# Fused attention and feed-forward kernel: one PSUM bank serves the attention scores first and layer one later

## The chip, the cores and the metric

The kernel runs on one core of one Trainium2 chip. The metric is the device time of one execution in microseconds (us); below the time, the traced span from the first to the last instruction is used, which is a little shorter. A difference is stated between medians of several executions.

The core has a matrix engine (TensorE, PE in the profile; loading its stationary operand is PEld), a vector engine (DVE), a scalar engine (ACT), a general engine (POOL) and a queue that issues the transfers (SP). Matrix products land in PSUM, which this kernel divides into eight banks of 128 partitions by 512 four-byte values.

## The reference, cut to what matters

```python
# 8 batches, 8 heads, 576 positions, head size 64
scores = q @ k.T / 8
cum    = cumsum(maximum(s, 0))
scores = where(causal, -1e9, scores + minimum(cum_k - cum_q, 0))
attn   = softmax(scores)
x      = (attn @ v) laid out as 4608 tokens x 512
h      = x @ w_in                      # 512 x 2048, "layer one"
g      = where(h > 0, h, exp(minimum(h, 0)) - 1)
out    = g @ w_out                     # 2048 x 512, "layer two"
```

## The kernel before

The program is written by a planner. Each piece of work is an `op` with a list of engines that could do it and what it costs there by a table, what it reads and writes, and a priority (smaller is more urgent). `Plan.issue` keeps a clock for each engine, repeatedly takes the operation that can start first (priority breaks ties) and appends its instructions. So the order on every engine is fixed when the program is built, each engine then runs its list in that order, and a small change in a rule reorders everything behind it. `plan.now` is the planned clock of TensorE. Times in the planner's table order the work; they aren't measurements.

**Attention** runs over batches and, within a batch, over pairs of heads `j` = 0 to 3. The first three batches begin with a *low* part of 320 positions in plain four-byte arithmetic (tiles `kl`, `ql`, `early`). A low unit makes five score tiles `sc` (one of 128 columns, two of 192, two of 320). A DVE instruction (L1144) adds the mask, takes the minimum `mn` and so frees the score bank; ACT exponentiates; the rows are normalised; then TensorE transposes them (`trl`), a copy brings them to `tl`, and the product with the values goes to `avl`. The remaining work, five whole batches and the late positions of the first three, splits operands in two parts (`sc<-kh,qs` and `sc<-k,q`), transposes by transfer (`T`), and has one small tile for each pair of heads and batch that covers the first 64 positions (names with `None`). The outputs become the tokens `x_first` (the first 512 tokens) and `x`.

**The network** takes 256 tokens at a time, 18 chunks. For each chunk it makes eight tiles `h` of layer one (two blocks of 128 features by 256 tokens, one PSUM bank), passes each through ACT and DVE to `g` and `gg`, and accumulates layer two in `o`. The first two chunks are native four-byte (L1447 and L1477, weights `wv`), the other sixteen use sums of three half-precision products (L1506 and L1566, weights `wp`). A chunk whose tokens come from two batches is first brought to one scale (L1411). The weights arrive as eight-byte words in `w_raw` and are decoded by ACT (L707) and DVE (L710 and L712), 1024 columns an instruction.

**Filler.** While the planned TensorE clock is under 60 us (`FILL_T`), a planned TensorE gap of more than 0.35 us (`GAP`) is filled with transposes of the identity into `scratch` (L1623), up to 300 of them. They compute nothing that is used.

**PSUM banks.** Eight are shared out by tags: `a` two (scores and transposes), `av` one, `h` three, `o` two. A tile may also name other tags with a rule; with `always=True` the planner may use them at any time the rule allows. Before, the score tiles name `h` and `o` under the rule `plan.now < OPEN_T`, and `OPEN_T` is 0.

Of the kernel before, what the change touches and what calls it, by code (L numbers as in the profile page):

```python
# [9 lines left out]
F32 = mybir.dt.float32  # L10
# [7 lines left out]
P = 128  # L18
# [6 lines left out]
SMALLEST = 2.0**-12  # L25
TOP, DOWN = 13, 22

N_ST, N_A, N_AV, N_H, N_O, N_IO, N_G, N_GG, N_X, N_T, N_K, N_V = 2, 2, 1, 3, 2, 2, 1, 3, 2, 2, 2, 2
TC = 256
NATIVE = 2  # L30
TX = 512
# [3 lines left out]

V_AHEAD = 30

FIRST_T, OPEN_T = 180e3, 0.0

DYN_T = 300e3  # L40

# [253 lines left out]
def pe4(n):  # L295

    return 4 * pe(n)
# [7 lines left out]
def act_c(n):  # L305

    return 165 + n / 1.2
# [36 lines left out]
def kernel(  # L344
# [39 lines left out]
    ps = ctx.enter_context(tc.tile_pool(name="ps", bufs=1, space=bass.MemoryType.PSUM))  # L384

    plan = Plan(tc)
# [183 lines left out]
    for n in range(NF // 2):  # L570
        tag = f"wa_{n}" if n < 4 else f"wp_{n // 2 - 1}"
# [8 lines left out]
    def weight(f, kind):  # L580
        t, at = w_values[f // 2]
        return (t, (f, kind)), lambda: t.v[:, at + f % 2, kind]
# [189 lines left out]
    for b, blocks in pieces:  # L772
        late = blocks[0] > 0
        start[b, late] = at
        n = P * len(blocks) + HB * (not late)
# [5 lines left out]
    def domains(ch):  # L781
# [5 lines left out]
                   others=[(f"wa_{m}", 1, lambda n: n > 0) for m in range(2)], always=True)  # L787
# [147 lines left out]
    def weighing_low(u):  # L935
        prio, n = u.prio + 1, CUT * P
        wide = P + 2 * n + sum(2 * (HB + P * i) for i in range(CUT))
        turned = plan.buf(sb, [P, wide], F32, f"tl_{u.tag}", tag="T", bufs=N_T)
        av = plan.buf(ps, [P, 512], F32, f"avl_{u.tag}", tag="av", bufs=N_AV)
        ends = [P]  # L940

        def pair():
            tr = plan.buf(ps, [P, 512], F32, f"trl_{u.tag}", tag="a", bufs=N_A)
            op(prio, [("PE", 111.0, lambda: pe_.transpose(tr.v[:, :P], u.first.v, ident))], [u.first], [tr],
               late=[low_scale[u.b]] if u.b in low_scale else ())
            psum_copy(prio, P, lambda: turned.v[:, :P], lambda: tr.v[:, :P], [tr], [(turned, "pair")])

            def products():
                for h in range(2):
                    pe_.matmul(av.v[h * HB : (h + 1) * HB, :HB], u.vs_of()[:, 0], turned.v[:, h * HB : (h + 1) * HB],  # L950
                               start=True, stop=True)

            op(prio, [("PE", 2 * pe4(HB), products)], [(turned, "pair"), u.vs], [av])

        def keys(kb):

            tr = plan.buf(ps, [P, 512], F32, f"trl_{u.tag}_{kb}", tag="a", bufs=N_A)
            i0, half = max(kb - 1, 0), kb > 0
            m, c = CUT - i0, P * (CUT - i0) - HB * half

            def turns():
                for h in range(2):
                    for i in range(i0, CUT):
                        o = (h * m + i - i0) * P
                        pe_.transpose(tr.v[:, o : o + P], u.pp[h, i].v[:, kb * P : (kb + 1) * P], ident)

            op(prio, [("PE", 222.0 * m, turns)], [u.pp[h, i] for h in range(2) for i in range(i0, CUT)], [tr],
               late=[low_scale[u.b]] if u.b in low_scale else ())
            at, = ends
            ends[0] = at + 2 * c  # L970

            def dst():
                return turned.v[:, at : at + 2 * c].rearrange("p (h q) -> p h q", h=2)

            psum_copy(prio, 2 * c, dst,
                      lambda: tr.v[:, : 2 * m * P].rearrange("p (h q) -> p h q", h=2)[:, :, m * P - c :],
                      [tr], [(turned, kb)])

            def products():
                for h in range(2):  # L980
                    pe_.matmul(av.v[h * HB : (h + 1) * HB, LOW - c : LOW], u.vs_of()[:, 1 + 2 * kb + h], dst()[:, h],
                               start=kb == 0, stop=kb == CUT)

            op(prio, [("PE", pe4(c), products)], [(turned, kb), u.vs], [av])
            if kb < CUT:
                return
            col = S_LOW + 2 * u.b
            produce(prio, u.j, start[u.b, False], LOW, lambda: av.v[:, :LOW],
                    [av] + ([(scales, col)] if u.b in low_scale else []),
                    lambda: scales.v[:, col : col + 1])  # L990

        return [pair] + [lambda kb=kb: keys(kb) for kb in range(CUT + 1)]
# [126 lines left out]

    plan.signal = (id(ps), "o")  # L1120

    def score_bank(name):

        def opening(n):
            return plan.now < OPEN_T

        return plan.buf(ps, [P, 512], F32, name, tag="a", bufs=N_A,
                        others=[("h", N_H, opening), ("o", N_O, opening)], always=True)

    def softmax_block(prio, tag, native, pt, w, mask, mv, reads, operands, inv, view=lambda v: v):  # L1130

# [297 lines left out]
    def network():  # L1429
# [10 lines left out]
        def hidden_native(ch, fp):  # L1440

            side = -1000
            hp = plan.buf(ps, [P, 2, TC], F32, f"h_{ch}_{fp}", tag="h", bufs=N_H)
            lo, up = ch * TC, ch * TC + TC
            for m in range(2):
                for c in range(NCB):
                    op(main(ch), [("PE", pe4(TC), lambda m=m, c=c: pe_.matmul(  # L1447
                        hp.v[:, m], weight(2 * fp + m, 0)[1]()[:, c * P : (c + 1) * P], x_first.v[:, c, lo:up],
                        start=c == 0, stop=c == NCB - 1))],
                       [(x_first, (j, a)) for a, e, j in x_spans if j == c and a < up and e > lo] + [weight(2 * fp + m, 0)[0]], [hp])  # L1450
            gt = plan.buf(sb, [P, 2 * TC], F32, f"g_{ch}_{fp}", tag="g", bufs=N_G)
            op(side, [("ACT", act_c(2 * TC), lambda: act.activation(gt.v, flat(hp.v), AF.Exp))], [hp], [gt])
            sign = [False]

            def negative():
                act.activation(gt.v, gt.v, AF.Relu, bias=1.0, scale=-1.0)
                sign[0] = True

            op(side, [
                ("DVE-SB", dve_1(2 * TC), lambda: dve.tensor_scalar(gt.v, gt.v, 1.0, -1.0, ALU.min, ALU.add)),  # L1460
                ("ACT", act_s(2 * TC), negative),
            ], [], [gt])
            gg = plan.buf(sb, [P, 2, TC], F32, f"gg_{ch}_{fp}", tag="gg", bufs=N_GG)
            op(side, [("DVE", dve_p(2 * TC), lambda: dve.scalar_tensor_tensor(
                flat(gg.v), flat(hp.v), 0.0, gt.v, ALU.max, ALU.subtract if sign[0] else ALU.add))],
               [gt, hp], [gg])
            return gg
# [19 lines left out]
        def hidden(n):  # L1487

            ch, fp = steps[n]
# [6 lines left out]
                group_constants(ch, cs[ch])  # L1496
            x, o = xs[ch * TC // TX], ch * TC % TX
            parts = [p for p in x_parts[ch * TC // TX] if p[0] < ch * TC + TC and p[1] > ch * TC]
            hp = plan.buf(ps, [P, 2, TC], F32, f"h_{ch}_{fp}", tag="h", bufs=N_H)
            for m in range(2):  # L1500
                f = 2 * fp + m
                for c in range(NCB):
# [202 lines left out]
```

## Time and profile before

| what | value |
|---|---|
| median of 3 runs | 1055.4 us (1053.96 to 1056.38) |
| the profiled execution: time, span | 1054.67 us, 1052.9 us |
| TensorE busy | 1031.1 us (98%) |
| DVE, ACT, POOL busy | 831.8, 623.3, 426.4 us |
| mean granted TensorE clock | 0.997 |

"Busy" for TensorE comes from modelled ends of matmuls that overlap in the pipeline, so the mean time of one is longer than the step from one to the next; where a price of one matmul is wanted, starts of successive rows are used. Filler counts as busy. A native four-byte matmul is recorded as two instructions.

### The profile page before, as it was taken

To read this page: it belongs to the slowest core of one execution; us is meant where nothing else is said; L and a number is where in the kernel's file an instruction comes from. 1 tells how busy PE (TensorE), PEld (TensorE's weight loads), DVE (VectorE), ACT (ScalarE), POOL (GpSimd) and SP (SyncE) were. 2 spreads that over 40 slices of the span, in tenths; PEclk is the share of its full clock that TensorE was granted. 3 is DMA by queue.
4 is the path that set the end of the run, shared out by engine and by line. 5 is a ranking of instruction groups with operands and counts; after the bars stand their busy time and mean duration, and the time that the engine had idled before them with its cause. 6 is when DMAs were issued, how large, how long until landed. Compare 5 with 4: busy or idle time off the path is not lost. (4 is left out here: it accounts for less than half of the span.)

```text
span 1052.9 us, 21378 instructions
## 1 busy us (share of the span) xinstructions
PE 1031.1 (98%) x7139; PEld 703.1 (67%) x7139; DVE 831.8 (79%) x2095; ACT 623.3 (59%) x1465; POOL 426.4 (40%) x671
## 2 busy tenths in 40 slices
PE   8999999999899999999999999999999999999998
PEld 6566566667567666766666666666676676766665
DVE  6898748998788889889888888789888888884333
ACT  4777555655566656766666666765565655653232
POOL 6322214445455435544554555563443424430000
PEclk9999999999899999999999999999999999999999
DMA  7776015656656666667656866685657565641000
GB/s 209 239 243 203 25 50 163 128 125 166 130 127 145 150 132 130 139 137 171 137 136 121 189 129 139 126 168 130 139 134 163 122 138 125 139 100 42 1 22 21
DMA packets 277823, 137.76 MB, mean 131 GB/s; under 512 B 211768, under 2 KB 255056, under 8 KB 277712
## 3 DMA queue, kind: packets, MB, share of 16 engines
q1 hardware_dynamic: 277712, 136.39, 56.2%
q8 instruction: 57, 0.93, 0.4%
q14 instruction: 54, 0.44, 0.1%
HBM read 70.22 MB, written 9.88 MB: 76 GB/s over the span
## 5 line engine op out<-in xcount | busy, mean ns | idle before, releaser
L1506 PE MATMUL h<-x,wp 128*128 128x256 f16 x3072 | 380.4, 274 | 5.4 <-DVE x L1411 4.7
L1566 PE MATMUL o<-wp,gg 128*128 128x512 f16 x1536 | 363.1, 380 | 0.0
L1506 PEld LDWEIGHTS <-wp 128*128 128x128 f16 x3072 | 288.6, 98 | 71.0 <-issue 15.8
L1566 PEld LDWEIGHTS <-gg 128*128 128x128 f16 x1536 | 143.7, 98 | 147.6 <-issue 4.0
L1149 ACT ACTIVATE p<-p,mn 128x192 f32<-128x192 f32 (+1 forms) x232 | 144.1, 621 | 85.4 <-DVE mn L1144 79.3
L1200 DVE SCALAR_TENSOR_TENSOR p<-p,sm,p 128x512 f16<-128x512 f32 (+3 forms) x231 | 164.2, 731 | 3.2 <-POOL p L1192 2.1
L1523 ACT ACTIVATE g<-h,cs 128x512 f32<-128x512 f32 x128 | 87.5, 683 | 94.0 <-PE h L1506 93.6
L1540 ACT ACTIVATE gg<-h,wc 128x512 f16<-128x512 f32 x117 | 80.1, 685 | 73.6 <-DVE h L1536 72.7
L1144 DVE CUSTOM_DVE_ANT_0 p<-sc,maskw 128x192 f32<-128x192 f32 (+1 forms) x232 | 109.6, 481 | 17.2 <-PE sc L1141 11.5
L1192 POOL TENSOR_SCALAR p<-p,sm 128x512 f16<-128x512 f32 (+3 forms) x116 | 72.8, 634 | 109.0 <-DVE sm L1155 73.5
L1141 PE MATMUL sc<-kh,qs 128*128 128x192 f32 (+2 forms) x272 | 112.2, 416 | 1.7 <-DVE mn L1144 0.8
L1545 DVE SCALAR_TENSOR_TENSOR gg<-h,wc,gg 128x512 f16<-128x512 f32 x128 | 95.5, 746 | 21.9 <-ACT gg L1540 21.3
L1536 DVE SCALAR_TENSOR_TENSOR h<-g,cs,h 128x512 f32<-128x512 f32 x128 | 96.2, 752 | 9.0 <-ACT g L1528 5.4
L1141 PE MATMUL sc<-k,q 128*128 128x192 f32 (+2 forms) x272 | 83.9, 312 | 0.8 <-POOL p L1192 0.4
L1532 DVE TENSOR_SCALAR g<-g 128x512 f32<-128x512 f32 x66 | 35.0, 530 | 59.4 <-ACT g L1523 58.9
L1196 ACT ACTIVATE p<-p,sm 128x512 f16<-128x512 f32 (+3 forms) x106 | 60.6, 592 | 13.4 <-DVE sm L1155 11.1
L1141 PEld LDWEIGHTS sc<-kh,qs 128*128 128x128 f32 x272 | 51.7, 190 | 22.5 <-DVE mn L1144 5.0
L424 POOL TENSOR_TENSOR qs<-stq,qs 64x512 fp32r<-64x512 f32 (+1 forms) x46 | 51.5, 1120 | 33.2 <-ACT qs L405 21.2
L1447 PE MATMUL h<-x_first,wv 128*128 128x256 f32 x256 | 63.5, 382 | 0.4 <-DVE x_first L431 0.4
L1477 PE MATMUL o<-wv,gg 128*128 128x512 f32 x128 | 63.1, 597 | 0.0
L1314 PE MATMUL av<-T,v 128*64 128x256 f16 (+5 forms) x896 | 60.6, 286 | 0.0
L1141 PEld LDWEIGHTS sc<-k,q 128*128 128x128 f32 x272 | 51.9, 191 | 4.8 <-issue 1.0
(190 smaller groups left out, 1403.7 us busy)
## 6 DMA issues: line engine op xcount, KB each, us to landing
stk<-in_kT_dram SPq DMA_DIRECT2D x64, 288.0 KB
stq<-in_qT_dram SPq DMA_DIRECT2D x40, 256.0 KB
va<-in_vb_dram SPq DMA_DIRECT2D x32, 320.0 KB
w_raw<-in_w_in_dram SPq DMA_DIRECT2D x16, 512.0 KB
w_raw<-in_w_out_dram SPq DMA_DIRECT2D x16, 512.0 KB
out_dram<-ost SPq DMA_DIRECT2D x32, 256.0 KB
q<-qs SPq DMA_DIRECT2D x40, 128.0 KB
T<-p SPq DMA_TRANSPOSE x208
```

What stands on the lines that cost most here:

```text
L1141: pe_.matmul(view(sc.v[:, :cw]), l, r, start=n == 0, stop=n == len(pairs) - 1)
L1144: op(prio, [("DVE", 84 + dve_p(cw), lambda i=i, sc=sc: dve.tensor_tensor_reduce(pt.v[:, i * cw : (i + 1) * cw], sc.v[:, :cw], mv(i * cw, c ...
L1149: op(prio, [("ACT", 480 + w / 1.2, lambda: act.activation(pt.v[:, :w], pt.v[:, :w], AF.Exp, bias=mn.v[:, n - 1 : n], scale=-1.0, accum_out ...
L1192: ("Pool", 160 + 1.04 * n, lambda part=part: pool.tensor_scalar(part(t16, 0), own(part), sm.v[:, r], 1.0, ALU.mult, ALU.mult)),
L1200: ("DVE-SB", dve_2(n), lambda part=part: dve.scalar_tensor_tensor(part(t16, 1), own(part), sm.v[:, r], part(t16, 0), ALU.mult, ALU.subtract)),
L1447: op(main(ch), [("PE", pe4(TC), lambda m=m, c=c: pe_.matmul(hp.v[:, m], weight(2 * fp + m, 0)[1]()[:, c * P : (c + 1) * P], x_first.v[:, c ...
L1506: pe_.matmul(hp.v[:, m], weight_part(f, 0, part)[1]()[:, c * P : (c + 1) * P], x.v[:, xx, c, o : o + TC], start=(c == 0 and i == 0), stop= ...
L1523: op(side, [("ACT", act_c(2 * TC) + 90, lambda: act.activation(gt.v, flat(hp.v), AF.Exp, scale=by(BACK)))], [hp, (cs[ch], g)], [gt])
L1536: op(side, [("DVE", dve_b(2 * TC), lambda: dve.scalar_tensor_tensor(flat(hp.v), gt.v, by(MINUS if sign[0] else FIRST), flat(hp.v), ALU.mul ...
L1540: ("ACT", act_c(2 * TC) + 90, lambda: act.activation(flat(gg.v[:, 0]), flat(hp.v), AF.Copy, scale=down())),
L1545: op(side, [("DVE", dve_b(2 * TC), lambda: dve.scalar_tensor_tensor(flat(gg.v[:, 1]), flat(hp.v), down(), flat(gg.v[:, 0]), ALU.mult, ALU. ...
L1566: pe_.matmul(acc[i].v, gg.v[:, a, m, i * P : (i + 1) * P], weight_part(2 * fp + m, 1, part)[1](), start=(first and m == 0 and k == 0), sto ...
```

## The change

Layer one's tag `h` goes from three banks to two, and a new tag `third` owns one bank. Score tiles, and now also the transposes `trl` of the low units, may use `third` besides `a` while the planned TensorE clock is under 165 us (`THIRD_T`); tiles of layer one may use it from then on. The unused `OPEN_T` rule goes. Decoding of the weights by 1024 columns is in both kernels: no line of the diff touches it. The order of the instructions on all engines is made anew. The lines of the functions below L1125 move down by seven, so L1141, L1144, L1411, L1506, L1566, L1623 are L1148, L1151, L1418, L1513, L1573, L1630 in the changed kernel.

```diff
-... N_H ... = ... 3 ...
+... N_H ... = ... 2 ...
-FIRST_T, OPEN_T = 180e3, 0.0
+FIRST_T, THIRD_T = 180e3, 165e3
...
         def pair():
-            tr = plan.buf(ps, [P, 512], F32, f"trl_{u.tag}", tag="a", bufs=N_A)
+            tr = score_bank(f"trl_{u.tag}")
...
         def keys(kb):
-            tr = plan.buf(ps, [P, 512], F32, f"trl_{u.tag}_{kb}", tag="a", bufs=N_A)
+            tr = score_bank(f"trl_{u.tag}_{kb}")
...
+    plan.tags[(id(ps), "third")] = 0
+
+    def first_stage(n):
+        return plan.now < THIRD_T
+
+    def second_stage(n):
+        return plan.now >= THIRD_T
+
+    def hidden_bank(name):
+        return plan.buf(ps, [P, 2, TC], F32, name, tag="h", bufs=N_H, others=[("third", 1, second_stage)], always=True)
+
     def score_bank(name):
-        def opening(n):
-            return plan.now < OPEN_T
-        return plan.buf(ps, [P, 512], F32, name, tag="a", bufs=N_A,
-                        others=[("h", N_H, opening), ("o", N_O, opening)], always=True)
+        return plan.buf(ps, [P, 512], F32, name, tag="a", bufs=N_A, others=[("third", 1, first_stage)], always=True)
...
-            hp = plan.buf(ps, [P, 2, TC], F32, f"h_{ch}_{fp}", tag="h", bufs=N_H)
+            hp = hidden_bank(f"h_{ch}_{fp}")
```

The last replacement is made twice, for the native chunks and for the others.

What the new order looks like is shown at three places. Names: `sc` a score tile, `trl` its transposes, `avl` a low unit's product, `h` layer one, `scratch` filler; the first number in a name is the head pair or the feature pair, the last is only a counter.

The first place is TensorE in the opening, at the third low unit (`sc_2`). Before, from the second score of that unit on:

```order
L1141 MATMUL sc_2_1_0_397<-early 128x192
L1623 MATMUL scratch<-ident 128x128 x2
L965 MATMUL trl_1_0_405<-ident,p_87 128x128
L965 MATMUL trl_1_0_405<-ident,p_176 128x128
L965 MATMUL trl_1_0_405<-ident,pl_0_1_171 128x128
L965 MATMUL trl_1_0_405<-ident,pl_0_1_178 128x128
L950 MATMUL avl_1_412<-tl_1_401,vs 64x64 x2
L1141 MATMUL sc_2_2_0_421<-early 128x192
```

After, the same place:

```order
L1148 MATMUL sc_2_1_0_364<-early 128x192
L1630 MATMUL scratch<-ident 128x128 x3
L1148 MATMUL sc_2_2_0_376<-early 128x192
L1630 MATMUL scratch<-ident 128x128 x5
L1148 MATMUL sc_2_3_0_390<-early 128x320
L944 MATMUL trl_1_396<-ident,pl_1_295 128x128
L1630 MATMUL scratch<-ident 128x128 x2
L965 MATMUL trl_1_0_404<-ident,p_87 128x128
```

The scores of a unit now stand ahead of the transposes of the unit before it, where before scores and transposes took turns. Over the whole program the filler rows sum to 120 transposes before and 87 after; TensorE's other instructions are the same in number and shape.

The second place is TensorE where the network's fourth chunk (chunk 3, the second on `x_855`, in the changed kernel `x_763`) begins. Its last 64 tokens come from `av_3_None`. Before:

```order
L1141 MATMUL sc_3_1_0_3_0_2963<-kh_3_1_0_2682,qs_3_1_0_2733 128x288
L1141 MATMUL sc_3_1_0_3_0_2963<-k_1_196,q_1_194 128x288
L1260 MATMUL av_3_None_2967<-pc_3_None_2792,vs_3_None_2463 128x128 x2
L1506 LDWEIGHTS wp_631
L1506 MATMUL h_0_2999<-x_855,wp_631 128x256
```

After, from the same product to the same matmul:

```order
L1267 MATMUL av_3_None_2874<-pc_3_None_2668,vs_3_None_2423 128x128 x2
L1148 MATMUL sc_3_1_0_2_0_2881<-kh_3_1_0_2607,qs_3_1_0_2652 128x448
L1148 MATMUL sc_3_1_0_2_0_2881<-k_1_195,q_1_193 128x448
...
L1148 MATMUL sc_0_None_0_2939<-khs_0_None_2658,qs_0_None_2750 128x128
L1148 MATMUL sc_0_None_0_2939<-k2s,q2s 128x128
...
L1573 MATMUL o_0_1_2411<-wp_2083,gg_2_2840 128x512
L1513 LDWEIGHTS wp_699
L1513 MATMUL h_0_2957<-x_763,wp_699 128x256
```

Between the product and the chunk's first matmul there was nothing; now there stand 12 matmuls of layer one and 12 of layer two of the chunk ahead, and four score tiles (448, 288, 288 and 128 columns). The third place is DVE there, before:

```order
L431 COPY xs_3_None_2974<-av_3_None_2967 64x64 x2
L1333 TENSOR_TENSOR xs_3_None_2974<-av_3_None_2967,xs_3_None_2974 64x64 x2
L1394 COPY cs_2981<-scales 128x1
L417 TENSOR_SCALAR x_855<-xs_3_None_2974,scales 128x64
L1421 TENSOR_SCALAR cs_2981<-scales,cs_2981 128x4
L1422 TENSOR_SCALAR cs_2981<-cs_2981 128x4
L621 TENSOR_SCALAR cs_2981<-cs_2981 128x4
L1424 TENSOR_TENSOR cs_2981<-cs_2981,wc 128x1
L832 SCALAR_TENSOR_TENSOR x_855<-xs_3_None_2974,scales,x_855 128x64
L1200 SCALAR_TENSOR_TENSOR p_3_3_0_0_3_2931<-p_176,sm_3_0_0_2843,p_3_3_0_0_3_2931 128x4x128
L1411 TENSOR_SCALAR x_855<-x_855,cs_1829 128x8x64
```

and after:

```order
L431 COPY xs_3_None_2886<-av_3_None_2874 64x64
L1151 ISA p_87,mn_3_1_0_2_2893<-sc_3_1_0_2_0_2881,maskw 128x448
L1151 ISA mn_3_1_0_2_2893 128x1
L1340 TENSOR_TENSOR xs_3_None_2886<-av_3_None_2874,xs_3_None_2886 64x64 x2
L1151 ISA p_176,mn_3_1_0_3_2917<-sc_3_1_0_3_0_2896,maskw 128x288
L1151 ISA mn_3_1_0_3_2917 128x1
L1151 ISA p_176,mn_3_1_0_3_2917<-sc_3_1_0_3_1_2913,maskw,mn_3_1_0_3_2917 128x288
L1151 ISA mn_3_1_0_3_2917 128x1
L832 SCALAR_TENSOR_TENSOR x_763<-xs_3_None_2886,scales,x_763 128x64
L1028 SCALAR_TENSOR_TENSOR v_0_0_0_2850<-va_1560,scales,v_0_0_0_2850 128x5x64
L1539 TENSOR_SCALAR g_3_2932<-g_3_2932 128x512
L1418 TENSOR_SCALAR x_763<-x_763,cs_1671 128x8x64
```

The next chunk's constants (`cs_2981`) have left the stretch, and three score minima have come in. Elsewhere on DVE, between the first and the ninth elementwise result of layer one (`gg`, L1464) there stand 189 rows before and 253 after: those between are mostly attention's. Of the sixteen weight decodes (L712) seven stand ahead of the first of these results before, and five after.

More of the change, by code (lines that the diff above doesn't have):

```diff
@@ L26 @@
 TOP, DOWN = 13, 22
-N_ST, N_A, N_AV, N_H, N_O, N_IO, N_G, N_GG, N_X, N_T, N_K, N_V = 2, 2, 1, 3, 2, 2, 1, 3, 2, 2, 2, 2
+N_ST, N_A, N_AV, N_H, N_O, N_IO, N_G, N_GG, N_X, N_T, N_K, N_V = 2, 2, 1, 2, 2, 2, 1, 3, 2, 2, 2, 2
 TC = 256
@@ L1498, in hidden @@
             parts = [p for p in x_parts[ch * TC // TX] if p[0] < ch * TC + TC and p[1] > ch * TC]
-            hp = plan.buf(ps, [P, 2, TC], F32, f"h_{ch}_{fp}", tag="h", bufs=N_H)
+            hp = hidden_bank(f"h_{ch}_{fp}")
             for m in range(2):
```

## The prediction, made before the changed kernel was run

> **What bounds the kernel now.** I read the page first, then TensorE's waits by stretch of time, then the timeline where a wait or filler stands.
>
> ```profile
> span 1052.9 us, 21378 instructions
> PE 1031.1 (98%) x7139; PEld 703.1 (67%) x7139; DVE 831.8 (79%) x2095; ACT 623.3 (59%) x1465; POOL 426.4 (40%) x671
> ...
> L1623 PE MATMUL scratch<-ident 128*128 128x128 f32 x120 | 17.0, 291 | 0.0
> ```
>
> TensorE is busy 98% of the span and idle 1052.9 - 1031.1 = 21.8 us. So the end is the useful work of TensorE, plus filler, plus idle time, plus what a slowed clock costs. The change leaves the useful matmuls as they are, in number and shape, so only the last three can move. The waits of TensorE in 0 to 60 us and in 200 to 320 us show what part of the idle time can go:
>
> ```profile
> PE sc L1141 <- DVE mn L1144: 1.4, 2, 1.0
> ...
> PE trl L965 <- DVE mn L1144: 0.3, 1, 0.3
> ...
> PE h L1506 <- DVE x L1411: 4.7, 1, 4.7
> PE h L1506 <- DVE gg L1545: 0.7, 1, 0.7
> PE sc L1141 <- DVE mn L1144: 0.7, 1, 0.7
> ```
>
> The reader is to see two things: scores that wait for `mn`, the instruction that frees a score bank, and one wait of 4.7 us for tokens, which no other comes near.
>
> **The change, part by part.**
>
> *Filler in the opening.* The program holds 120 filler transposes before and 87 after, 33 fewer. The price is the step from one to the next where filler runs undisturbed; the rows behind it are for the work that filler covers:
>
> ```profile
> 33.41 2.13 PE L1623 MATMUL scratch<-ident 128*128 128x128 f32 x18
> 35.41 0.33 PE L944 MATMUL trl<-ident,pl 128*128 128x128 f32 x1
> ...
> L712 DVE SCALAR_TENSOR_TENSOR wv<-w_raw 128x1024 uint32<-128x1024 uint32 x16 | 19.9, 1245 | 0.5
> L710 DVE TENSOR_SCALAR w_raw<-w_raw 128x1024 uint32<-128x1024 uint32 x16 | 11.5, 716 | 0.4 <-DMA w_raw<-in_w_out_dram 0.4
> ...
> L1144 DVE CUSTOM_DVE_ANT_0 p<-sc,maskw 128x448 f32<-128x448 f32 x64 | 39.5, 617 | 1.6 <-PE sc L1141 1.2
> ```
>
> 18 of them take 35.41 - 33.41 = 2.00 us, 0.111 each, so 33 take 3.7 us. That is saved only if TensorE does not wait in its place. What filler covers is one low unit after another on DVE, and DVE has less other work ahead of the first `gg` than before: five weight decodes instead of seven, 2 x (1.25 + 0.72) = 3.9 us less, against three more score minima at 0.62 or less, 1.9 us. By this view DVE gets there 2.0 us earlier at least, and by the filler 3.7. The ends are 0 (filler is only replaced by waits) and 3.7. I take 3.7: the filler rows count TensorE's gaps directly, and maxima and copies moved too, which the two kinds of rows leave out.
>
> *A third score bank.* The waits of the opening for a bank are 1.4 + 0.3 = 1.7 us. With one more bank a score waits for the minimum three tiles back. I take -1.7, with ends 0 and -1.7.
>
> *The wait of 4.7 us.* TensorE's timeline there, with the wait ahead of a row in brackets, and its windows (stretch, length, busy time, granted clock, share and rate of transfers):
>
> ```profile
> 271.33 0.33 PE L1260 MATMUL av_None<-pc_None,vs_None 128*128 128x128 f32 x2
> 276.36 1.44 PE L1506 MATMUL h<-x,wp 128*128 128x256 f16 x6 [4.70 <-DVE x L1411]
> 277.45 0.59 PE L1141 MATMUL sc<-kh,qs 128*128 128x288 f32 x1
> ...
> 275.00:280.00 5.00, 3.64 (x17) 0.52 0.21 57
> 280.00:285.00 5.00, 5.00 (x39) 0.80 0.91 141
> ```
>
> TensorE made the last product that chunk 3 needs and had nothing else in its list until DVE had turned it into scaled tokens. Behind the wait the clock is low: six matmuls took 277.45 - 276.36 = 1.09 us. At full clock the steps are these, from the chain of the last stage and the timeline at 405 us:
>
> ```profile
> 1020.08 2.62 PE h L1506 x24
> 1022.70 2.59 PE o L1566 x12
> ...
> 405.22 0.37 PE L1141 MATMUL sc<-kh,qs 128*128 128x448 f32 x1
> ...
> 405.64 1.48 PE L1506 MATMUL h<-x,wp 128*128 128x256 f16 x12
> 406.88 0.38 PE L1141 MATMUL sc<-kh,qs 128*128 128x288 f32 x1
> ...
> 407.24 0.83 PE L1506 MATMUL h<-x,wp 128*128 128x256 f16 x6
> ```
>
> One matmul of layer one steps by 2.62 / 24 = 0.109 us, one of layer two by 2.59 / 12 = 0.216; six of the first should have taken 0.65. By the windows the clock cost 0.48 x 3.64 + 0.20 x 5.00 = 2.7 us. So this place is worth 4.7 + 2.7 = 7.4 us.
>
> After the change there is cover between that product and the chunk's first matmul: 12 of layer one (1.31 us), 12 of layer two (2.59), score tiles of 448 columns (405.64 - 405.22 = 0.42), 288 and 288 (0.36 each) and 128 (at about 0.3, estimated from the 288): 5.3 us. The need before was 4.7. On DVE it changes:
>
> ```profile
> 272.94 0.22 DVE L1421 TENSOR_SCALAR cs<-scales,cs 128x4 f32<-128x4 f32 x1
> ...
> 273.94 1.24 DVE L1424 TENSOR_TENSOR cs<-cs,wc 128x1 f32<-128x1 f32 x1
> ...
> L1200 DVE SCALAR_TENSOR_TENSOR p<-p,sm,p 128x512 f16<-128x512 f32 x127 | 107.9, 866 | 1.3 <-POOL p L1192 0.6
> ...
> L1532 DVE TENSOR_SCALAR g<-g 128x512 f32<-128x512 f32 x66 | 35.0, 530 | 59.4 <-ACT g L1523 58.9
> ...
> L1028 DVE SCALAR_TENSOR_TENSOR v<-va,scales,v 128x320 f16<-128x320 f32 x32 | 20.0, 640 | 0.0
> ```
>
> The next chunk's constants go, 273.94 + 1.24 - 272.94 = 2.2 us, and one L1200 of 0.9; three minima (0.62 or less), a `v` (0.64) and a `g` (0.53) come, 3.0 us. That makes 4.7 - 3.1 + 3.0 = 4.6 us, under the 5.3. Those minima are the other half of the cover: the score tiles in it need banks, which the minima free. I take -7.4; the ends are 0 (the wait is as it was) and -7.4.
>
> [...]
>
> *DVE from the first to the ninth result of layer one.* Running attention ahead asks for DVE's work earlier. Between those results (`gg`, L1464) DVE's list has 189 rows before and 253 after. The rows are DVE's, then DVE's windows (busy time behind the length), the sum of its windows from 40 to 80 us, and TensorE's first use of each result and its busy time between:
>
> ```profile
> 58.57 0.68 DVE L1464 SCALAR_TENSOR_TENSOR gg<-h,g 128x512 f32<-128x512 f32 x1
> 148.64 0.69 DVE L1464 SCALAR_TENSOR_TENSOR gg<-h,g 128x512 f32<-128x512 f32 x1
> ...
> 58.57:90.62 32.05, 28.27 (x74) 1.00 0.71 234
> 90.62:119.51 28.89, 24.25 (x75) 1.00 0.37 120
> 119.51:148.64 29.13, 14.92 (x48) 1.00 0.11 34
> ...
> sum 40.00, DVE 37.74; mean DVE 9.44
> ...
> 59.92 1.02 PE L1477 MATMUL o<-wv,gg 128*128 128x512 f32 x2
> 153.44 1.02 PE L1477 MATMUL o<-wv,gg 128*128 128x512 f32 x2
> ...
> 59.00:151.00 92.00, 90.75 (x442) 1.00 0.39 128
> ```
>
> DVE worked 28.27 + 24.25 + 14.92 = 67.4 us there; at the same mean per row 253 rows are 67.4 x 253 / 189 = 90.3 us. TensorE took 153.44 - 59.92 = 93.5 us, nearly all busy. Its list between the two uses grows from 197 rows to 216; it will need 93.5 if the added rows are the short ones, 102.5 in proportion, and I take the middle, 98. So DVE, 75% busy there before, must be 92% busy. At the rate of 40 to 80 us, 37.74 / 40 = 94%, it needs 95.7 us and TensorE waits for nothing; at the 88% of the first window it needs 102.6 and TensorE waits 4.6. I take 1.5 us of waits, nearer the first end, since 40 to 80 us has the same mix of decodes and low units; the ends are 0 and 4.6.
>
> *The rest.* The bank goes back to layer one at 165 us of planned time; from then on both kernels share out the banks alike. The other waits quoted (0.7 and 0.7, and 92.00 - 90.75 = 1.25 up to 151 us), 2.7 us, may fall or move: 0, with ends of 2.7 either way. The last output is the same work. Decoding by 1024 columns is in before already (the row of L712) and costs nothing new.
>
> *The sum.* -3.7 - 1.7 - 7.4 + 1.5 = -11.3 us. Against the profiled execution, 1054.67 us with 1.8 us of it outside the span, that is 1043.4; the median shown is 0.7 higher, so 1044 against 1055.4.
>
> **Rivals.**
>
> *One of the two gains fails.* Either the filler is only replaced by waits (left: -7.4 + 1.5 = -5.9, 1049.5 us), or chunk 3 waits as before, or a wait of that length appears elsewhere and takes the clock with it (left: -3.7 - 1.7 + 1.5 = -3.9, 1051.5 us). For it: the cover of 5.3 exceeds the chain of 4.6 by only 0.7 us. Against it: a remainder of half a microsecond is an eighth of the wait that had the slow clock behind it.
>
> *Nothing is gained.* Both fail, and the banks only swap who waits: 1055.4 + 1.5, about 1057, or the same within noise. For it speaks that filler follows DVE more than banks; against it, that the cover of chunk 3 stands in the order.
>
> *DVE becomes the bound, and the kernel slower.* If DVE can be busy a share u of that stretch, it takes 90.3 / u. The gains of 12.8 us are eaten when 90.3 / u = 98 + 12.8, at u = 0.815. At 0.80 it takes 112.9 us, TensorE waits 14.9, and the time is 1055.4 - 12.8 + 14.9 = 1057.5. For it: the mean before was 75%. Against it: DVE then waited for a TensorE that had no break, and reached 94% when it had work.
>
> *Layer one loses its cover with two banks.* A tile of `h` then waits until `gg` of the tile two back is done. Eight native tiles in 93.5 us are one in 11.7 us, and the emptying (exponent, one more pass, `gg`) must fit between. It would have to overrun by 11.3 / 16 = 0.7 us on each of the 16 native tiles to eat the gain, and by 0.9 for 1058. [...] Against it: no wait quoted is of `h` for a bank, and an instruction of the emptying takes 0.5 to 0.7 us.
>
> **How the numbers follow.** A change of 0.2%, 2.1 us, is about what a measurement of this kernel can tell from none. The forecast, both gains (1039 to 1049), has 0.64; one gain fails (1049 to 1053.3) 0.16; nothing gained (1053.3 to 1057.5) 0.09; slower through DVE 0.08, through layer one's banks 0.03. So faster 0.80, same 0.09, slower 0.11. The lower end is the sum without the 1.5 and the small waits, 1044 - 1.5 - 2.7 = 1039.8, taken as 1039 for the 0.7 between execution and median. The range goes up to 1054, which leaves out slightly under 0.2.
>
> **What would show it.** In the profile after: 87 filler transposes at about 0.11; no `sc` waiting for `mn` in the opening; no wait of `h` for L1418 above 1 us and no dip of the clock at 260 to 280 us; DVE above 90% busy between the first and ninth `gg`, and TensorE's waits there 1 to 2 us together. The prediction is wrong if TensorE's idle time outside filler in the first 60 us grows by over 3 us, if a wait for `gg`, `wv` or `mn` of over 4 us stands between 60 and 200 us, or if the matmul of chunk 3 still waits.

## The result and the profile after

The changed kernel took 1037.9 us (median of 4, 1037.24 to 1038.33) where the kernel before took 1054.7 beside it: a ratio of 0.9838, interval 0.9821 to 0.9856. The forecast was 1044 with a range from 1039: the sign was right, the time lies 1 us below the range, and some 5 us of the gain were not foreseen. The profiled execution took 1038.24 us with a span of 1036.5, 16.4 less than before.

First the page: the span, the engines, and the filler's group.

```profile
span 1036.5 us, 21332 instructions
PE 1019.3 (98%) x7106; PEld 703.1 (68%) x7106; DVE 838.6 (81%) x2092; ACT 610.0 (59%) x1439; POOL 435.7 (42%) x695
...
L1630 PE MATMUL scratch<-ident 128*128 128x128 f32 x87 | 13.6, 305 | 0.0
```

TensorE's busy time fell by 11.8 us, its idle time from 21.8 to 1036.5 - 1019.3 = 17.2. Filler takes 3.4 of the 11.8. Then TensorE's waits: two of the opening (0 to 60 us), two of 60 to 200, two of 200 to 320 (waiting tile, releaser, total us, how often, longest).

```profile
PE sc L1148 <- DVE tl L431: 1.0, 1, 1.0
PE sc L1148 <- DVE mn L1151: 0.7, 2, 0.4
...
PE sc L1148 <- DVE mn L1151: 2.1, 3, 1.7
PE trl L944 <- POOL pl L1167: 0.6, 1, 0.6
...
PE o L1573 <- DVE gg L1552: 0.2, 1, 0.2
PE h L1513 <- DVE x L1418: 0.2, 1, 0.2
```

The wait of 4.7 us for chunk 3's tokens is 0.2. In the opening the waits for a score bank fell from 1.7 to 0.7, but a wait of 1.0 for `tl` came. The windows in which chunk 3 now begins, with the end of its cover on TensorE and two rows of DVE's chain, and then those of the stretch from the first to the ninth use of `gg`, with TensorE's rows for the two uses and DVE's window from the first `gg` to the ninth (53.6 to 153.24 us):

```profile
255.00:260.00 5.00, 5.00 (x37) 3.63 (x36) 4.29 (x15) 4.20 (x13) 4.77 (x9) 1.00 0.87 186
260.00:265.00 5.00, 4.77 (x36) 3.27 (x33) 4.94 (x12) 3.55 (x9) 1.84 (x3) 1.00 0.50 121
...
255.64 0.41 PE L1148 MATMUL sc<-kh,qs 128*128 128x448 f32 x1
261.15 2.78 PE L1513 MATMUL h<-x,wp 128*128 128x256 f16 x24 [0.23 <-DVE x L1418]
...
258.80 1.71 DVE L1028 SCALAR_TENSOR_TENSOR v<-va,scales,v 128x320 f16<-128x320 f32 x1
260.76 0.34 DVE L1418 TENSOR_SCALAR x<-x,cs 128x512 f16<-128x512 f16 x1
```

```profile
57.04 1.02 PE L1484 MATMUL o<-wv,gg 128*128 128x512 f32 x2
154.80 1.02 PE L1484 MATMUL o<-wv,gg 128*128 128x512 f32 x2
57.04:154.80 97.76, 94.53 (x479) 1.00 0.56 174
...
53.60:153.24 99.64, 92.69 (x263) 1.00 0.54 171
```

In the windows of the first fence the columns are TensorE's busy time, then that of PEld, DVE, ACT and POOL, then the granted clock: it is 1.00 there, and 1.000 in the mean of the whole execution. The stretch takes 97.8 us: TensorE is busy 94.5 of them, where 98 were forecast, and idle 97.76 - 94.53 = 3.2, against 1.25 before and 1.5 more forecast. DVE is busy 92.69 / 99.64 = 93% of its own.

**Where the rest is.** Take filler and the loss by the slow clock out of TensorE's busy time, and what is left is the useful matmuls at full clock: before 1031.1 - 17.0 - 2.7 = 1011.4 us, after 1019.3 - 13.6 = 1005.7. The same matmuls, in number and shape, got 5.7 us shorter. Their order shows where. A low unit's products with the values (`avl`) have 64 columns on the stationary side, their neighbours 128. In the lists of TensorE the `avl` stood in 47 separate groups before, in 33 after. (The late products `av` have 64 columns too; they stand in 32 groups in both.) Two rows of TensorE's timeline for each group of one low unit, before and then after (the row behind a group gives its end):

```profile
38.48 0.65 PE L981 MATMUL avl<-tl,vs 128*64 128x256 f32 x4
39.07 0.59 PE L1141 MATMUL sc<-early 128*128 128x192 f32 x2
...
41.00 0.55 PE L981 MATMUL avl<-tl,vs 128*64 128x192 f32 x4
41.48 0.33 PE L965 MATMUL trl<-ident,p 128*128 128x128 f32 x1
...
42.60 0.34 PE L981 MATMUL avl<-tl,vs 128*64 128x64 f32 x4
42.87 0.49 PE L1141 MATMUL sc<-kl,ql 128*128 128x128 f32 x2
```

```profile
45.12 1.09 PE L981 MATMUL avl<-tl,vs 128*64 128x256 f32 x12
46.15 1.22 PE L1148 MATMUL sc<-kl,ql 128*128 128x128 f32 x4
```

The same twelve instructions take 0.59 + 0.48 + 0.27 = 1.34 us in three groups and 1.03 in one. The change of width ahead of a group shows in the step before it:

```profile
49.79 1.03 PE L1454 MATMUL h<-x_first,wv 128*128 128x256 f32 x4
50.75 0.34 PE L950 MATMUL avl<-tl,vs 128*64 128x64 f32 x4
```

Elsewhere such a matmul of layer one steps by 0.216 (eight in 49.04 - 47.31 = 1.73 us). Four are 0.86; the products start 0.96 behind them, about 0.1 late. So the theory for the missing 5 us was: going to 64 stationary columns and back costs TensorE about 0.19 us, and the third bank let transposes stand together, so that products did too. The rival: the forecast's terms are all there is, and they were only sized too small.

### The profile page after: what moved, and what is told of

It reads as the page before. It is cut to its first block, busy times and chain, and to the rows that moved or that the text cites. A ratio compares the mean times of both kernels' runs of the same rounds, so it can differ in the third digit from the quotient of the medians.

```text
span 1036.5 us, 21332 instructions
## 1 busy us (share of the span) xinstructions
PE 1019.3 (98%) x7106; PEld 703.1 (68%) x7106; DVE 838.6 (81%) x2092; ACT 610.0 (59%) x1439; POOL 435.7 (42%) x695
## 4 chain that ended last, share of the span: by engine, by line
PE 86%; DVE 8%; DMA 2%; issue 1%; POOL 1%; ACT 1%; SPq 1%; POOLq 0%; DVEq 0%
PE o L1573 30%; PE h L1513 30%; PE sc L1148 9%; PE av L1321 6%; PE o L1484 4%; PE h L1454 4%; DMA w_raw<-in_w_out_dram 1%; DVE p L1207 1%; PE avl L981 1%; PE trl L965 1%; DVE p L1151 1%; DVE peaks L613 1%; PE scratch L1630 1%; DVE wp L747 1%; SPq L391 0%
## 5 line engine op out<-in xcount | busy, mean ns | idle before, releaser
L1513 PE MATMUL h<-x,wp 128*128 128x256 f16 x3072 | 379.0, 273 | 0.2 <-DVE x L1418 0.2
L1573 PE MATMUL o<-wp,gg 128*128 128x512 f16 x1536 | 362.9, 379 | 1.4 <-DVE gg L1552 1.4
L1513 PEld LDWEIGHTS <-wp 128*128 128x128 f16 x3072 | 286.8, 98 | 61.5 <-issue 8.8
L1573 PEld LDWEIGHTS <-gg 128*128 128x128 f16 x1536 | 144.7, 98 | 150.4 <-issue 4.7
L1207 DVE SCALAR_TENSOR_TENSOR p<-p,sm,p 128x512 f16<-128x512 f32 (+3 forms) x225 | 160.0, 736 | 2.9 <-POOL p L1199 1.5
L1151 DVE CUSTOM_DVE_ANT_0 p<-sc,maskw 128x192 f32<-128x192 f32 (+1 forms) x232 | 109.1, 481 | 19.4 <-PE sc L1148 17.1
L1199 POOL TENSOR_SCALAR p<-p,sm 128x512 f16<-128x512 f32 (+3 forms) x118 | 78.5, 673 | 96.9 <-DVE sm L1162 54.5
L1148 PE MATMUL sc<-kh,qs 128*128 128x192 f32 (+2 forms) x272 | 112.3, 416 | 2.7 <-DVE mn L1151 2.7
L1148 PE MATMUL sc<-k,q 128*128 128x192 f32 (+2 forms) x272 | 83.6, 311 | 0.6 <-DMA q<-qs 0.6
L1148 PEld LDWEIGHTS sc<-kh,qs 128*128 128x128 f32 x272 | 51.6, 190 | 22.8 <-DVE mn L1151 5.7
L424 POOL TENSOR_TENSOR k<-stk,kh 64x576 fp32r<-64x576 f32 x40 | 59.3, 1481 | 18.3 <-ACT kh L405 15.0
L1484 PE MATMUL o<-wv,gg 128*128 128x512 f32 x128 | 60.8, 594 | 0.0
L403 POOL TENSOR_SCALAR qs<-stq 128x512 fp32r<-128x512 f32 (+1 forms) x40 | 24.2, 604 | 81.0 <-PE sc L1148 63.6
```

Source lines behind the costliest of these rows:

```text
L1148: pe_.matmul(view(sc.v[:, :cw]), l, r, start=n == 0, stop=n == len(pairs) - 1)
L1151: op(prio, [("DVE", 84 + dve_p(cw), lambda i=i, sc=sc: dve.tensor_tensor_reduce(pt.v[:, i * cw : (i + 1) * cw], sc.v[:, :cw], mv(i * cw, c ...
L1207: ("DVE-SB", dve_2(n), lambda part=part: dve.scalar_tensor_tensor(part(t16, 1), own(part), sm.v[:, r], part(t16, 0), ALU.mult, ALU.subtract)),
L1484: op(main(ch), [("PE", pe4(DM), lambda i=i, m=m: pe_.matmul(acc[i].v, gg.v[:, m, i * P : (i + 1) * P], weight(2 * fp + m, 1)[1](), start=f ...
L1513: pe_.matmul(hp.v[:, m], weight_part(f, 0, part)[1]()[:, c * P : (c + 1) * P], x.v[:, xx, c, o : o + TC], start=(c == 0 and i == 0), stop= ...
L1573: pe_.matmul(acc[i].v, gg.v[:, a, m, i * P : (i + 1) * P], weight_part(2 * fp + m, 1, part)[1](), start=(first and m == 0 and k == 0), sto ...
```

## Experiments

All medians stand beside runs of the kernel before on the same chip (1054.7, 1055.9, 1055.3 and 1055.5 us in the four sets). To compare over chips the ratios are used; 0.001 is 1.05 us.

**Who needs the third bank?** First the transposes are sent back to the two banks they had:

```diff
-            tr = score_bank(f"trl_{u.tag}")
+            tr = plan.buf(ps, [P, 512], F32, f"trl_{u.tag}", tag="a", bufs=N_A)
```

(and the same for the other transposes of a low unit).

> Only the scores of the opening may use the third bank; the transposes of the low units keep to the two banks they had. By the plan 90 fillers (87 after the change, 120 before), the cover ahead of chunk 3 is 5.25 us as after the change, and TensorE's four-byte instructions stand in 499 uninterrupted groups (500 after, 553 before). If the whole gain comes from filler, the wait of chunk 3 and a fixed cost of about 0.1 us per group of four-byte instructions: 3.3 + 7.4 + 5.4 = 16.1 us under before, 1038.6. If groups cost nothing and the forecast's terms hold: about 1044. If the third bank served through the transposes: near 1048.

1037.0 us, ratio 0.9828 (0.9805 to 0.9851): the whole gain. The mirror image leaves the scores on two banks:

```diff
-            sc = score_bank(f"sc_{tag}_{i}")
+            sc = plan.buf(ps, [P, 512], F32, f"sc_{tag}_{i}", tag="a", bufs=N_A)
```

> Only the transposes of the low units may use the third bank; the scores keep to two. By the plan 123 fillers, the cover of chunk 3 stays 5.25 us, groups of four-byte instructions 518. With a cost of 0.1 us per group: +0.3 - 7.4 - 3.5 = 10.6 under before, 1044. By the forecast's terms without a cost of groups: 1047.3. If chunk 3 waits as before: 1052 or more, with a row of h waiting 4 us or more for L1418.

1044.1 us, 0.9902 (0.9882 to 0.9922): no filler saved, chunk 3 without its wait (0.2 for L1418), 39 groups of products. So the scores alone bring the whole gain, and the transposes alone some 10 of the 17 us. In the first of the two kernels the products stand in 32 groups though their transposes have only two banks; that the scores have left them these two is the likely reason, which no run shows by itself.

**Nobody uses it, or for a shorter or longer time.** The rule for the first stage returns `False`:

> The changed kernel, but nobody may use the third bank in the opening: scores and transposes have two, and layer one has two until 165 us of planned time. By the plan 122 fillers, 551 groups as before, cover of chunk 3 is 1.99 us. If layer one does as well with two banks as with three there: the wait of chunk 3 falls to 2 to 3 us and with it the slow clock, 4.8 us under before, about 1050. If two banks cost layer one its cover: 1054 or more, with waits of h for gg. If any wait there slows the clock as before: 1053.

1053.7 us, 0.9990 (0.9976 to 1.0003): not the 1050 of the first case. The second and the third number lie within the interval, and the trace shows something of both. Chunk 3 begins without a wait, but behind 48 matmuls of layer one, at 282.6 us, its next tile waits for `gg`, and a slow clock follows. The wait, and the windows there (length, TensorE's busy time, clock):

```profile
PE h L1513 <- DVE gg L1552: 2.3, 1, 2.3
...
280.00:285.00 5.00, 2.75 (x12) 0.75 0.50 122
285.00:290.00 5.00, 5.00 (x34) 0.91 0.96 198
```

A wait half as long as before, 2.3 us, still had a slow clock behind it. From 60 to 200 us no `h` waits for `gg` in this kernel, so two banks cost layer one nothing visible in the native chunks. Then the hand-over, `THIRD_T`, at 60, 250 and 400 us of planned time:

> The changed kernel with the bank handed to layer one at 60 us of planned time instead of 165. Fillers 87, as after; cover of chunk 3 by the plan 3.3 us instead of 5.25; 536 groups of four-byte instructions instead of 500. By a cost of 0.1 us per group: 3.7 for filler + 6.0 for chunk 3 (a wait of 1.4, too short to slow the clock) + 1.7 for groups = 11.4 under before, 1043.4. By the forecast's terms without groups: 1045. If the gain comes from the opening before 60 us alone: 1049.

1047.4 us, 0.9924 (0.9900 to 0.9948): by the ratio some 3 us more than the first number and 2 less than the last. The interval leaves out only the first. That a wait of 1.4 us is too short to slow the clock was the author's estimate. The profile after had waits up to 1.7 us between its matmuls with the clock at 1.00; this run waited 2.3 us up to 277 us, and behind that windows of 1 us read 0.50 from 278 to 280. No run shows where a limit lies.

> The changed kernel with the bank handed over at 250 us of planned time. Fillers 87, cover of chunk 3 by the plan 10.5 us, 492 groups. By a cost of 0.1 us per group: 0.8 us better than the change, about 1037. If more work ahead only makes DVE late, so that TensorE waits for layer one's results: 1040 or more.

1045.5 us, 0.9913 (0.9890 to 0.9936).

> The changed kernel with the bank handed over at 400 us of planned time. Fillers 87, cover of chunk 3 by the plan 12.6 us, 491 groups. By a cost of 0.1 us per group: 0.9 us better than the change, about 1037. If layer one loses its cover with two banks, it is lost for 235 us more here and the time rises to 1042 or more, with waits of h for gg.

1043.9 us, 0.9889 (0.9869 to 0.9908). The last two are worse than the change, not better: each came out at the worse number of its expectation. TensorE's waits for layer one's banks between 200 and 320 us, in the runs with 60, 250 and 400:

```profile
PE h L1513 <- DVE gg L1552: 2.3, 1, 2.3
```

```profile
PE h L1513 <- DVE gg L1552: 1.8, 1, 1.8
```

```profile
PE h L1513 <- DVE gg L1552: 3.7, 4, 1.8
```

In the changed kernel no such wait stands there. The half-precision chunks begin at 212 us. With the bank still at the scores, both late kernels wait 1.8 us for `gg` at 222 us, and the one with 400 waits three times more; 165 us hands the bank back in time for that. The wait with 60 is another: layer one has had its third bank for long there, and the wait stands at 277 us, as with the idle bank behind 48 matmuls of layer one with little else among them. So the rival "layer one loses its cover with two banks" was priced for the native tiles, where it did not happen, and it is real one stage later, with 1.8 to 3.7 us. These waits are less than the 5 to 8 us that the two kernels lost; the rest was not traced.

**Is it the number of groups?** In the changed kernel each transpose of a low unit is made to wait for the unit's previous product (added to its `late` list), so the old turns come back:

> The changed kernel, but each transpose of a low unit waits for the unit's previous product, so that transposes and products take turns again. Fillers 85 by the plan, cover of chunk 3 as after, groups of four-byte instructions 541 instead of 500. If a group costs about 0.1 us, this gives 2 to 4 us back: 1040 to 1042. If groups cost nothing: 1038, as after the change, and the rows of the products av of low units stay at their mean of after.

1043.4 us, 0.9893 (0.9872 to 0.9913): 5.8 us back by the ratios, more than expected. The group of products in this run, and in the changed kernel:

```profile
L982 PE MATMUL avl<-tl,vs 128*64 128x256 f32 (+2 forms) x144 | 18.9, 341 | 1.4 <-DVE tl L431 1.3
```

```profile
L981 PE MATMUL avl<-tl,vs 128*64 128x256 f32 (+2 forms) x144 | 15.3, 323 | 0.1
```

3.6 us more in the same 144 instructions, which stand in 48 groups here and in 33 there. The profile in turns also lost 2.7 us to a slow clock in the opening, which the profile after did not. So the runs show the direction, and the rows a size near 0.25 us for each of the 15 groups.

**The price of a change of width by itself.** A dummy of 64 moving columns goes ahead of each of the 128 half-precision tiles of layer one, into the tile's own bank, and is overwritten. The plan does not know of it, so the order stays. Only the stationary width differs between the first two kernels:

```diff
+                        for _ in range(1 if m == 0 and c == 0 else 0):
+                            pe_.matmul(hp.v[:128, 0, :HB], weight_part(f, 0, 0)[1]()[:, :128],
+                                       x.v[:, 0, 0, o : o + HB], start=True, stop=True)
```

(128 becomes 64 in the second kernel, and the count becomes 2 in the third.)

> The changed kernel with one dummy matmul added ahead of each of the 128 f16 tiles of layer one, 64 moving columns against a stationary side of 128 columns, like its neighbours. Its own work is 64 columns at 0.42 ns, 0.03 us. Every theory: 128 x 0.03 = 3.5 us over the changed kernel, about 1041. It is the control for the next two.

1043.2 us, 0.9884 (0.9861 to 0.9908): by the ratios 4.9 us over the changed kernel where 3.5 were expected, a difference that the intervals cover.

> The same 128 dummies at the same places, but with a stationary side of 64 columns, as the products of attention have. If TensorE pays about 0.19 us for each change to 64 stationary columns and back (0.093 going in and 0.100 coming out in the steps of the trace after): 128 x 0.19 = 24.7 us over the run with 128 columns, about 1066. If the width costs nothing and the shorter useful time has another cause: as the run with 128 columns, about 1041.

1067.4 us, 1.0108 (1.0086 to 1.0130): 24.2 us over the control, 0.189 us for each dummy (by the intervals of the ratios 0.16 to 0.21).

> The changed kernel with two dummies of 64 stationary columns, one behind the other, ahead of each of the 128 f16 tiles of layer one, instead of one. If the price belongs to the change of width: 128 x 0.03 = 3.5 us over the run with one, about 1071. If it belongs to each instruction of 64 columns: 24 us over it, about 1091.

1071.1 us, 1.0151 (1.0132 to 1.0170): the second dummy costs 3.7 us in all (4.5 by the ratios, as the two kernels ran on two chips), about its own work (128 x 64 columns at 0.42 ns, the step of layer two over its 512, are 3.5) and far from 24. So the price belongs to the change of width. Two places of one kind in TensorE's timeline, in the first and in the second kernel:

```profile
654.14 1.47 PE L1576 MATMUL o<-wp,gg 128*128 128x512 f16 x6
655.44 0.19 PE L1513 MATMUL h<-x,wp 128*128 128x64 f16 x1
655.47 0.49 PE L1516 MATMUL h<-x,wp 128*128 128x256 f16 x3
```

```profile
625.07 1.46 PE L1576 MATMUL o<-wp,gg 128*128 128x512 f16 x6
626.46 0.22 PE L1513 MATMUL h<-x,wp 128*64 128x64 f16 x1
626.61 0.50 PE L1516 MATMUL h<-x,wp 128*128 128x256 f16 x3
```

From the six matmuls of layer two to the dummy it is 1.30 us, then 1.39; from the dummy to layer one 0.03, then 0.15. So at this place it is 0.09 us going in and 0.12 coming out; over the 128 it is 0.19 on average. No run here shows what TensorE does within the step. The prediction had no term for a change of width.

**Grouping more.** In the changed kernel the four products of a low unit become one operation behind its last transpose:

```diff
+        held = []
...
-            op(prio, [("PE", pe4(c), products)], [(turned, kb), u.vs], [av])
+            held.append(products)
             if kb < CUT:
                 return
...
+            op(prio, [("PE", 2 * pe4(HB) + 2 * pe4(2 * CUT * HB), all_products)],
+               [(turned, part) for part in ("pair", *range(CUT + 1))] + [u.vs], [av])
```

> The changed kernel with the four products of a low unit issued as one group behind its last transpose. Groups of 64-column products of low units fall from 33 to 12, fillers 85. If a group costs 0.19 us for its two changes of width: 21 x 0.19 = 4.0 us, and 0.2 of filler, under the changed kernel, about 1034. If the width costs nothing: as the changed kernel, 1038. If the later product delays the unit's result and TensorE waits for it: 1038 or more, with waits for tl in the first 160 us.

1034.2 us, 0.9794 (0.9769 to 0.9819), as the price said. The low units' products in the kernel before (47 groups; 33 after had 15.3 us) and in this one (12 groups):

```profile
L981 PE MATMUL avl<-tl,vs 128*64 128x256 f32 (+2 forms) x144 | 18.2, 333 | 0.0
```

```profile
L982 PE MATMUL avl<-tl,vs 128*64 128x256 f32 (+2 forms) x144 | 12.5, 309 | 0.0
```

With the third bank for scores alone, beside the changed kernel on one chip:

> The changed kernel with both: third bank for scores alone, products of a low unit as one group. Groups of products 12 as in the run with grouping, fillers 83 instead of 85. By filler and width it is 0.2 us better than grouping alone, 1034; if the transposes need the third bank once they all come ahead of the products: 1035 or more, with waits for tl.

> The changed kernel itself on the chip of the three runs beside it, so that grouping is compared on one chip: 1038, and the run with grouping and the bank for scores alone 4 us under it if a group costs 0.19 us.

1036.0 us, 0.9819 (0.9801 to 0.9838), against 1039.8, 0.9854 (0.9837 to 0.9872), for the changed kernel: 3.8 us better where 4 were expected, though no better than grouping alone, and without waits for `tl`. Grouping alone has no run beside the changed kernel on one chip; by the ratios it is 4.6 us better. So grouping beats both kernels of the case. The same edit in the kernel before:

> The kernel before, without the third bank, with the four products of a low unit as one group behind its last transpose. Groups of products fall from 47 to 12, fillers rise from 120 to 146, the cover of chunk 3 is 2.0 us instead of 0.3. By the change of width: 35 x 0.19 = 6.6 less, 2.9 more for filler, and 0 to 4.8 less at chunk 3 (the run with the bank left idle had the same cover and gained about 1): about 1050, between 1046 and 1051. If the changes of width cost nothing: 1055 to 1058.

1057.9 us, 1.0016 (1.0002 to 1.0031): a miss by 8 us. The profiled execution took 1061.1, the longest of the twelve. Its page and its filler:

```profile
span 1059.3 us, 21427 instructions
...
PE 1027.9 (97%) x7164; PEld 711.7 (67%) x7164; DVE 846.2 (80%) x2111; ACT 615.9 (58%) x1448; POOL 425.9 (40%) x666
...
L1631 PE MATMUL scratch<-ident 128*128 128x128 f32 x145 | 21.0, 289 | 0.0
```

and its wait of chunk 3:

```profile
PE h L1514 <- DVE x L1419: 3.0, 1, 3.0
```

The useful time is 1027.9 - 21.0 - 5.1 for the slow clock (three stretches, by the windows (0.17 + 0.02 + 0.15) x 10 + (0.14 + 0.20) x 5) = 1001.8 us, 9.6 less than before. But idle time is 1059.3 - 1027.9 = 31.4 (21.8 before), filler 4.0 longer, and chunk 3 waits 3.0. The cheaper order was bought with waits. That a product at the end of its unit leaves TensorE less to do in between, and that without the third bank there are no scores to put there, is a reading of the order which no run tests by itself.

**Does the clock fall because TensorE stands still?** The kernel before, with dummy transposes into the bank of chunk 3's first tile while it waits. In the first version the plan counted their time:

> The kernel before with 36 dummy transposes added into the first layer-one bank of chunk 3, placed where TensorE waits 4.7 us for tokens. They need 4.0 us at full clock and let TensorE work while the wait lasts. If the slow clock behind the wait costs 2.7 us because TensorE stood still, the time falls by 2 to 3 us, to about 1052, and the granted clock stays at 1.0 from 270 to 290 us. If the clock falls for another reason, the time stays at 1054.7 or rises by what the dummies overrun.

1055.5 us, 0.9999 (0.9984 to 1.0014). The clock stayed at 1.00 there, but the plan's later order had changed with it (waits for `mn` behind 320 us went from 0.2 to 2.9 us), so this decided nothing. The second version gives them no planned time, and every other row of TensorE's list stays:

```diff
+            if ch == 3 and n % (NF // 2) == 0:
...
+                    for _ in range(40):
+                        pe_.transpose(flat(hp.v)[:, :P], ident, ident)
+                op(main(ch), [("PE", 0.0, keep_warm)], [], [hp], late=[gate[N_WHOLE, NP - 1]])
```

> The kernel before with 40 dummy transposes in the wait of chunk 3 and everything else in the same order (the run with 36 dummies had moved later work). They take 4.4 us of the 4.7 us wait. If the clock falls because TensorE stands still: the granted clock stays at 1.0 and the kernel is 2.5 us faster than before, 0.9976 of its time. If the slow clock has another cause: 1.000, with a slow window at 275 to 285 us as before.

1051.2 us, 0.9957 (0.9944 to 0.9971): 4.0 us faster. The place in its timeline, and its windows:

```profile
273.43 4.55 PE L1505 MATMUL h<-ident 128*128 128x128 f32 x40
278.31 0.82 PE L1513 MATMUL h<-x,wp 128*128 128x256 f16 x6 [0.32 <-DVE x L1413]
...
275.00:280.00 5.00, 4.68 (x42) 1.00 0.89 148
280.00:285.00 5.00, 5.00 (x48) 1.00 0.55 121
```

The wait is as long as before, filled, and the clock does not fall there. The gain is above the 2.5 expected: over the 17 runs of the kernel before on that chip the mean granted clock was 0.9956, over the 12 of this one 0.9992, and 0.0036 of 1053 us is 3.8. So one profiled execution had understated what the slow clock costs over many; where the others lost it is not on record.

## Why the prediction was right and wrong, point by point

The account of the span is: idle time -4.6, filler -3.4, slow clock -2.7, useful matmuls -5.7, together -16.4. The last is what the other three leave.

- *Filler, -3.7 forecast.* -3.4 in the filler's group, with 87 of them. Held.
- *Third score bank, -1.7.* The waits for `mn` fell by 1.0, others came, and TensorE's idle time of the first 60 us went from 6.8 to 6.3. About -0.5: too large by 1.2. The sign "no `sc` waiting for `mn` in the opening" did not come, since 0.7 us is left.
- *The wait of 4.7 us and its clock, -7.4.* 4.5 of the wait went and 2.7 of the clock: -7.2 in the profiled pair. Held, and the dummies confirm the clock's part, but with no margin. The cover runs from 255.64 us to 0.23 us ahead of 261.15, 5.3 us as forecast. The wait left behind it says that DVE's chain took 5.5 and not 4.6: its `v` alone took 1.71 us where 0.64 was forecast. "One of the two gains fails" fell, and "nothing is gained" with it.
- *DVE between the first and the ninth `gg`, +1.5.* TensorE's idle time there rose by 2.0, to 3.2 where the signs named 1 to 2, and DVE is busy 93% (92% forecast). TensorE's own work is 94.5 us, though, not the 98 taken as the middle between two ends, so that the term came out near is in part luck. The longest wait is of a score for `mn` (1.7), not of layer two for `gg`. DVE did not become the bound.
- *The rest, 0 with ends of 2.7.* All other idle time: -4.6 + 0.5 + 4.5 - 2.0 = -1.6. Inside.
- *"The change leaves the useful matmuls as they are, in number and shape, so only the last three can move."* This is the step that failed: it put a term of -5.7 us at nothing. Number and shape stayed, their neighbours did not. How much of it is the groups can be read from starts. For each group of `avl`, take the time from the start of the matmul ahead of it to the start of the one behind it, without the step that the first has elsewhere (a median) and without recorded waits and the slow clock, and add up over the trace. That gives 15.03 us in the run with grouping (12 groups), 20.48 after (33), 23.84 before (47) and 24.27 in turns (48). So a group costs about 0.25 us in the four-byte low units, rather more than the 0.19 of the half-precision dummies, and the 14 groups less are 3.4 us of the 5.7. Of the rest, 1.3 us are in the steps of matmuls directly ahead of a recorded wait (5.7 us over their usual steps before, 4.4 after): idle time that "busy" counts. About 1 us was not traced. Useful time alone is a rough measure of this, since it is 1011.4 us at 47 groups and 1024.1 - 13.1 - 2.7 = 1008.3 at 48.
- *Grouping, foretold at 0.19 us a group.* The time came out right partly by luck: by the starts its 21 groups less are 5.5 us and not 4.0, and TensorE's idle time rose by 0.9, from 17.2 to 18.1.

The rows that should have warned were in the trace of before: `avl` groups of four instructions whose length did not follow their columns, 0.59 us for 256 and 0.27 for 64, and the line through the two leaves 0.16 us for no columns at all.

The prediction's 2.7 us for the slow clock is what the windows of before show as missing while TensorE was busy. Over their whole length 0.48 x 5 + 0.20 x 5 = 3.4 us are missing, and windows of 1 us read 0.50 from 276 to 282 us:

```profile
276.00:277.00 1.00, 0.64 (x4) 0.50 0.04 12
...
281.00:282.00 1.00, 1.00 (x6) 0.50 0.50 106
```

So the clock was at half for 3.4 / 0.50 = 6.8 us. In the kernel with the idle bank 0.25 x 5 + 0.09 x 5 = 1.7 us are missing, 3.4 us at half:

```profile
283.00:284.00 1.00, 1.00 (x5) 0.50 0.66 131
284.00:285.00 1.00, 1.00 (x4) 0.50 0.24 61
```

In these two the longer wait, 4.7 us against 2.3, had the longer slow stretch behind it; what sets its length no run shows.

## What to carry to other kernels

The same matmuls in another order are not the same work: count the changes between stationary widths on TensorE (here 0.19 us there and back, and about 0.25 in the four-byte low units) before calling useful time constant, and put the narrow products of a unit into one group if there is other work to fill the time until they can start (here 1034.2 us with the third bank, 1057.9 without). A bank pays where the list is short of work to run ahead with, and only until its first owner needs it: handed back 105 us of planned time earlier, or 85 or 235 later, a third to a half of the gain was lost. A wait on the busiest engine costs more than its length when a slow clock follows (here 2.7 us more behind 4.7), and what the clock costs is read from several executions, not from one (here the dummies gained 4.0 us where one profile showed 2.7).

## What was not expected of the hardware

- A change between 128 and 64 stationary columns and back costs 0.19 us (24.2 us for 128), and a second instruction of the same width costs about its own columns (3.7 us for 128).
- A wait of 2.3 us had a slow clock of 3.4 us behind it in the kernel with the idle bank; waits up to 1.7 us between the matmuls of the profile after had none (1.00 in its windows). Length alone may not decide it: the run with grouping waited 2.1 us at 153 us without one (1.00 from 150 to 160 us).
- With no line of the kernel changed, the mean granted clock of the kernel before lay between 0.992 and 0.998 over its runs, which is 2 to 8 us of its time.
